# Longer rows for w_mod, w_gate and the last 4 MB of w_o in a decode layer whose loads never stop

## The chip, the cores and the metric

The kernel runs on one core of a Trainium2 chip. The metric is the device time of one execution in microseconds (us), median over runs. "Span" is the profiled execution from its first to its last instruction, some 1.4 us less than the device time (436.2 us at 437.56, before).

## The reference, cut to what matters

One token goes through one transformer layer: adaLN modulation, attention with 32 query heads and 4 cached key/value heads of 65,536 positions, and a gated feed-forward network.

```python
# x, c: (1, 1024); w_mod: (1024, 6144); wq: (1024, 4096); wo: (4096, 1024)
# k_cache, v_cache: (4, 65536, 128); w_gate, w_up: (1024, 3584); w_down: (3584, 1024); all bf16
mod = silu(c) @ w_mod                       # six vectors sa, ca, ga, sb, cb, gb
h = layernorm(x) * (1 + ca) + sa
x = x + ga * (attention(h @ wq, k_cache, v_cache) @ wo)
h = layernorm(x) * (1 + cb) + sb
return x + gb * ((gelu(h @ w_gate) * (h @ w_up)) @ w_down)
```

The arithmetic is small. What has to be moved is not: 67 MB of K, 67 MB of V and 51 MB of weights, 185.6 MB in all, each byte read once.

## The kernel before

All large loads go through one queue (SyncE) into ten slots of 16 KB per partition. A load is planned with the slots it takes; `issue_ready` sends the loads off in their order, each as soon as the last users of its slots are done. Nearly every load has a partition's bytes as one contiguous run in memory, called a row below (some of w_down are two): a load of 2 k-rows of w_mod is 128 rows of 24 KB.

```python
    def plan_load(src, view_fn, slot, site=None, nslot=1, beside=None, off=0, sem=None):

        if site is not None:
            site.n += 16
            tok = (site.sem, site.n)
        else:
            sem = slot if sem is None else sem
            nfill[sem] += 1
            tok = (fill[sem], 16 * nfill[sem])
        job = Job(view_fn(slot_all[:, slot * SLOT + off:(slot + nslot) * SLOT]), tok, slot)
        job.src = src
        job.freed = None
        job.prev = []
        if beside is not None:
            job.prev = beside.prev
        for t in range(slot, slot + (nslot if beside is None else 0)):
            if last_job[t] is not None and last_job[t] not in job.prev:
                job.prev.append(last_job[t])
            last_job[t] = job
        loads.append(job)
        return job

    # ... (cut)

    def issue_ready():

        while issued[0] < len(loads):
            j = loads[issued[0]]
            if any(q.freed is None for q in j.prev):
                return
            SP.wait(*(q.freed for q in j.prev))
            sp.dma_start(j.view, j.src).then_inc(j.tok[0], 16)
            issued[0] += 1
# ... (cut)
        head = iter([8, 0, 2, 4, 6, 8])
        j_mod = [(plan_load(wmod_v[:, k:k + 2, :], flat(2, M6), next(head), nslot=2), k, 2) for k in range(0, KD, 2)]
        j_q = [(plan_load(wq_v[:, k:k + 4, :], flat(4, HQ * DH), next(head), nslot=2), k, 4) for k in range(0, KD, 4)]
        tail = iter([2, 4, 6, 8])
        tail_d = iter([0, 1, 2, 3, 4, 5])

        def plan_o(k, slot):
            return (plan_load(wo_v[:, k:k + 8, :], flat(8, D), slot), k, 8)
        # ... (cut: K and V in loads of 4 MB, 128 rows of 32 KB)
        j_o += [plan_o(16, 0), plan_o(24, 1)]
        j_g = [(plan_load(wg_v[:, k:k + 4, :], flat(4, F), next(tail), nslot=2), k, 4) for k in range(0, KD, 4)]
        j_u = [(plan_load(wu_v[:, k:k + 4, :], flat(4, F), next(tail), nslot=2), k, 4) for k in range(0, KD, 4)]
```

w_mod is four loads, wq two, w_o four, w_gate two. wq's second half takes the slots of w_mod's first piece. K then goes to slots 0 to 3 and V to slots 4 to 7. Slot 5 is read once before anything of V has landed (multiplied by zeros), so the part of it that w_mod does not cover is cleared by a memset on GpSimd.

The matrix products with weights all go through one helper. It waits for one load, does all matmuls on it, and releases the slots:

```python
        def row_matvec(place, jobs, pad, ready, last_k, between=None):

            PE.wait(*ready)
            tok = None
            seen = set()
            for n, (jb, view, k0, nk) in enumerate(jobs):
                PE.wait(jb.tok)
                ins = None
                for kk in range(nk):
                    k = k0 + kk
                    for out, c0 in place(k):
                        ins = pe.matmul(
                            out, pad[:, k, :], view[:, kk, c0:c0 + ROW],
                            start=k <= last_k[0], stop=k >= last_k[1], skip_group_check=True,
                        )
                tok = PE.done(ins)
                release(jb, tok)
                if n == 0 and between is not None:
                    between()
            return tok
```

Of the kernel before, what the change touches and what calls it, by code (L numbers as in the profile page):

```python
# [10 lines left out]
SLOT = 8192  # L11
NSLOT = 10
SITES = 4
# [5 lines left out]
UE = 4  # L19
# [61 lines left out]
def bass_adaLN_cond__gqa_block_cached__geglu_ffn__decode_kernel(  # L81
# [14 lines left out]
    D = A_x.shape[-1]  # L96
    KD = D // P
# [6 lines left out]
    F = B_w_gate.shape[1]  # L104
    FD = F // P
    M6 = w_mod.shape[1]
# [4 lines left out]
    NB = CH // TB  # L111
    scale = float(DH) ** -0.5
    NQ = P // QD
    assert FD % UE == 0 and M6 <= SLOT and KD % 4 == 0
    assert REP * NB == QD and NB == NQ and CH == NB * NQ * (ROW // P) and HQ == QD
    assert D == 2 * ROW and HQ * DH == 2 * NQ * ROW and F % ROW == 0 and F <= 2 * NQ * ROW and UE * P == ROW

# [5 lines left out]
    sp, pe, dve, act, pool = nc.sync, nc.tensor, nc.vector, nc.scalar, nc.gpsimd  # L123
# [68 lines left out]
    slots = [slot_all[:, i * SLOT:(i + 1) * SLOT] for i in range(NSLOT)]  # L192
# [7 lines left out]
# [21 lines that stand above are left out]
# [20 lines left out]
    def flat(nk, n):  # L241
        return lambda t: t[:, 0:nk * n].rearrange("p (k n) -> p k n", k=nk)

    def emit_all():
# [3 lines left out]
        wmod_v = w_mod.rearrange("(p k) n -> p k n", p=P)  # L248
        wq_v = A_wq.rearrange("(p k) n -> p k n", p=P)
        wo_v = A_wo.rearrange("(p k) n -> p k n", p=P)  # L250
        wg_v = B_w_gate.rearrange("(p k) n -> p k n", p=P)
# [5 lines left out]
        def kv_src(h, i, n=1):  # L257
            g, cc = divmod(i, NCH)
            return h[g][:, cc * CH:(cc + n) * CH, :]

        head = iter([8, 0, 2, 4, 6, 8])
        j_mod = [(plan_load(wmod_v[:, k:k + 2, :], flat(2, M6), next(head), nslot=2), k, 2) for k in range(0, KD, 2)]
        j_q = [(plan_load(wq_v[:, k:k + 4, :], flat(4, HQ * DH), next(head), nslot=2), k, 4) for k in range(0, KD, 4)]
        tail = iter([2, 4, 6, 8])
        tail_d = iter([0, 1, 2, 3, 4, 5])

        def plan_o(k, slot):
            return (plan_load(wo_v[:, k:k + 8, :], flat(8, D), slot), k, 8)

        def vslot(j):  # L270
            return SITES + j % SITES
# [10 lines left out]
        j_o = []  # L282
        for i in range(0, NC + KU, KU):
            if i < NC:
                j_k[i] = plan_load(kv_src(kh, i, KU), flat(KU * CH, DH), i % SITES, kfill[i % SITES // KU], KU)
            if i == SITES - KU:
                j_o.append(plan_o(0, 8))
            if i == NC:
                j_o.append(plan_o(8, 9))
            if i >= KU:  # L290
                j = i - KU
                j_v[j] = plan_load(kv_src(vh, j, VU), flat(VU * CH, DH), vslot(j), vfill[j % SITES // VU], VU)
        j_o += [plan_o(16, 0), plan_o(24, 1)]
        j_g = [(plan_load(wg_v[:, k:k + 4, :], flat(4, F), next(tail), nslot=2), k, 4) for k in range(0, KD, 4)]
        j_u = [(plan_load(wu_v[:, k:k + 4, :], flat(4, F), next(tail), nslot=2), k, 4) for k in range(0, KD, 4)]
        j_d = []
        NBF = FD // UE
# [43 lines left out]
        pool.memset(p_row[:, :, :], 0.0)  # L341
        pool.memset(p_sb[:, :, :], 0.0)
        pool.memset(m_sp[:, :, :], 0.0)
        pool.memset(slots[SITES + 1][:, 2 * M6 - SLOT:SLOT], 0.0)
        for a in [a for r in ev for a in r] + ex + m1 + oc + pc + kfill + vfill:
            pool.sem_inc(a.sem, a.unit)
        v_zero = GP.done(pool.memset(kt_sb[:, 1, :, :], 0.0))
# [531 lines left out]
        assert issued[0] == len(loads)  # L879

    emit_all()
    return nc

# [27 lines left out]
```

## Time and profile before

| | before |
|---|---|
| device time | 437.57 us (3 runs, 437.57 to 437.58) |
| span of the profiled run | 436.2 us |
| bytes on the load queue | 185.60 MB in 8176 packets |
| busy: TensorE, DVE, ScalarE | 69%, 47%, 26% |
| DMA engines | 99.0% of the span under load packets |

The page's lines are quoted and read in the prediction below. Two habits of reading help here. First, the DMA row is in tenths per slice, so a 9 means 90% or more, and the row under it, GB/s, shows what moved. Second, a load counts as landed when the last of 16 DMA engines has reported. The views show that last report ("us to landing", or the end of a wait). For the last piece of w_mod it comes at 32.69 us, and the matmuls that wait for it start at 32.73. With 128 rows to a load, that is 8 rows for each engine, and the last reports of the four pieces of w_mod (10.92, 18.18, 25.44 and 32.69 us) are 7.25 or 7.26 us apart, about 8 times the 0.912 us that one of their packets takes.

### The profile page before, as it was taken

Reading aid. Unit: us, or ns where it says so; the run is one execution under the profiler, and the core shown is the slowest. Engines: PE = TensorE matmul, PEld = TensorE weight load, DVE = VectorE, ACT = ScalarE, POOL = GpSimd, SP = SyncE. Lnnn points to the kernel's source line nnn. Section 1 sums busy time; section 2 is a strip of 40 time slices with the busy share of each in tenths; the row PEclk is TensorE's granted clock in tenths of the full one; section 3 lists DMA queues with packets and bytes.
Section 4 is the critical chain, followed back from the end, with each engine's and each line's share of the span. In section 5 each row is a group of like instructions: output and inputs, shape, how many; then the busy total and the mean of one; then the engine's idle time right before and its main releaser. Section 6 shows DMA issues by size and latency. Waiting matters only on the chain.

```text
span 436.2 us, 8423 instructions
## 1 busy us (share of the span) xinstructions
PE 302.8 (69%) x3858; PEld 200.5 (46%) x3858; DVE 206.7 (47%) x303; ACT 111.2 (26%) x164; POOL 16.8 (4%) x23
## 2 busy tenths in 40 slices
PE   0435559959696878949787794969689596565366
PEld 0112236736464656636465563646456373232024
DVE  6601015637373755736474763738377465321001
ACT  1000001533332423333341353333235334000000
POOL 9500000000000000000000000000000000000000
PEclk9995569999796988988896897969689889578856
DMA  8999999999999999999999999999999999999996
GB/s 355 433 421 434 433 431 431 431 432 433 433 433 439 430 433 433 436 433 433 439 433 433 433 430 436 433 436 436 433 433 433 433 418 436 437 433 429 420 425 265
DMA packets 8192, 185.77 MB, mean 426 GB/s; under 512 B 1010, under 2 KB 1010, under 8 KB 1652
## 3 DMA queue, kind: packets, MB, share of 16 engines
q1 hardware_dynamic: 8176, 185.60, 99.0%
q8 instruction: 8, 0.13, 0.1%
q14 instruction: 4, 0.03, 0.0%
q10 hardware_dynamic: 4, 0.00, 0.0%
HBM read 185.60 MB, written 0.00 MB: 426 GB/s over the span
## 4 chain that ended last, share of the span: by engine, by line
DMA 56%; PE 31%; DVE 11%; issue 1%; ACT 1%; POOL 0%; POOLq 0%
DMA slots<-in_A_k_cache_dram 45%; PE kt_ps L575 16%; DMA slots<-in_B_w_down_dram 7%; PE b L645 4%; DMA slots<-in_A_v_cache_dram 4%; PE sc_ps L597 4%; PE kt_ps L409 3%; DVE selt L359 3%; DVE kt_sb L683 2%; DVE s_pad L717 1%; DVE o_red L706 1%; PE sc_ps L626 1%; PE b L613 1%; PE b L386 1%; DVE o_acc L694 1%
## 5 line engine op out<-in xcount | busy, mean ns | idle before, releaser
L575 PE MATMUL kt_ps<-ident,slots 128*128 128x128 bf16 x2048 | 156.7, 238 | 48.8 <-DMA slots<-in_A_k_cache_dram 48.0
L683 DVE COPY kt_sb<-kt_ps 128x2048 bf16<-128x2048 bf16 x96 | 117.6, 1225 | 111.5 <-PE kt_ps L575 109.9
L575 PEld LDWEIGHTS kt_ps<-ident,slots 128*128 128x128 bf16 x2048 | 136.1, 108 | 74.3 <-issue 41.9
L683 ACT ACTIVATE kt_sb<-kt_ps 128x2048 bf16<-128x2048 bf16 x32 | 60.1, 1877 | 27.7 <-PE kt_ps L575 27.7
L732 ACT ACTIVATE p_sb<-sc_ps 128x512 bf16<-128x512 bf16 x32 | 19.1, 597 | 182.4 <-PE sc_ps L626 182.4
L597 PE MATMUL sc_ps<-kt_sb,q_buf 128*32 128x512 bf16 x528 | 50.8, 420 | 0.0
L645 PE MATMUL b<-slots,p_sb 128*32 128x512 bf16 x560 | 40.1, 411 | 5.3 <-DMA slots<-in_A_v_cache_dram 4.6
L409 PE MATMUL kt_ps<-slots,h_pad 128*32 128x512 bf16 x176 | 19.1, 571 | 22.0 <-DMA slots<-in_B_w_up_dram 9.7
L694 DVE SCALAR_TENSOR_TENSOR o_acc<-o_acc,s_pad,b 128x512 f32<-128x512 f32 x28 | 20.9, 747 | 12.2 <-PE b L645 11.9
L613 PE MATMUL b<-m_sp,selt 128*128 128x16 f32 x66 | 13.0, 272 | 18.2 <-DVE m_sp L722 16.5
L645 PEld LDWEIGHTS b<-slots,p_sb 128*32 128x32 bf16 x560 | 15.5, 104 | 20.1 <-issue 5.1
L717 DVE TENSOR_REDUCE s_pad<-sc_ps 128x1 f32<-128x512 f32 x32 | 21.8, 682 | 0.0
L738 ACT ACTIVATE p_row<-sc_ps,s_pad 128x512 bf16<-128x512 f32 x32 | 21.7, 677 | 0.0
L409 PEld LDWEIGHTS kt_ps<-slots,h_pad 128*32 128x32 bf16 x176 | 6.3, 130 | 32.7 <-issue 11.9
L613 PEld LDWEIGHTS b<-m_sp,selt 128*128 128x128 f32 x66 | 9.8, 188 | 23.7 <-DVE m_sp L722 21.4
L597 PEld LDWEIGHTS sc_ps<-kt_sb,q_buf 128*32 128x32 bf16 x528 | 10.9, 95 | 12.3 <-issue 4.5
L409 PE MATMUL kt_ps<-slots,s_pad 128*32 128x512 bf16 x96 | 10.9, 516 | 7.5 <-DMA slots<-in_w_mod_dram 7.5
L452 POOL TENSOR_TENSOR rs<-va,halfneg 128x1 f32<-128x1 f32 x2 | 1.1, 555 | 375.7 <-DVE va L449 375.7
L793 DVE COPY kt_sb<-kt_ps 128x512 f32<-128x512 f32 x3 | 2.1, 692 | 27.7 <-PE kt_ps L409 27.7
L626 PEld LDWEIGHTS sc_ps<-ident,p_row 128*128 128x128 bf16 x136 | 7.8, 98 | 15.1 <-issue 14.4
L626 PE MATMUL sc_ps<-ident,p_row 128*128 128x128 bf16 x136 | 13.7, 224 | 0.2 <-ACT p_row L738 0.2
L727 DVE TENSOR_REDUCE s_pad<-b 128x1 f32<-128x16 f32 x32 | 5.6, 175 | 14.6 <-PE b L613 14.6
(98 smaller groups left out, 148.1 us busy)
## 6 DMA issues: line engine op xcount, KB each, us to landing
slots<-in_A_k_cache_dram SPq DMA_DIRECT2D x16, 4096.0 KB, 23.5
slots<-in_A_v_cache_dram SPq DMA_DIRECT2D x16, 4096.0 KB, 23.6
slots<-in_w_mod_dram SPq DMA_DIRECT2D x4, 3072.0 KB, 20.4
slots<-in_A_wq_dram SPq DMA_DIRECT2D x2, 4096.0 KB, 35.8
slots<-in_A_wo_dram SPq DMA_DIRECT2D x4, 2048.0 KB, 25.3
slots<-in_B_w_gate_dram SPq DMA_DIRECT2D x2, 3584.0 KB, 30.2
slots<-in_B_w_up_dram SPq DMA_DIRECT2D x2, 3584.0 KB, 29.5
slots<-in_B_w_down_dram SPq DMA_DIRECT2D x2, 2048.0 KB, 35.1
```

Of the source, the lines that this page charges most:

```text
L359: dve.tensor_scalar(selt[:, :].rearrange("p (r h) -> p r h", h=REP), selw[:, HQ - REP:HQ].unsqueeze(1).to_broadcast([P, NR, REP]), -scale, ...
L409: ins = pe.matmul(out, pad[:, k, :], view[:, kk, c0:c0 + ROW], start=k <= last_k[0], stop=k >= last_k[1], skip_group_check=True,)
L575: ins = pe.transpose(kt_ps[:, half * 2048 + t * P:half * 2048 + (t + 1) * P], j_k[i - i % KU].view[:, i % KU * CH + b * TB + t, :], ident[ ...
L597: ins = pe.matmul(sc(j)[QD * g:QD * (g + 1), :], q_buf[:, j % SITES, QD * b:QD * (b + 1)], kt_sb[:, j % 2, n:n + w, :].rearrange("p n d -> ...
L613: ins = pe.matmul(b6[:, 0:NR], selt[:, :], m_sp[:, j % 2, :], start=True, stop=True)
L626: ins = pe.transpose(sc_bf[:, o:o + P], p_row[:, j % 2, c * P:(c + 1) * P], ident[:, :])
L645: ins = pe.matmul(b7[QD * c:QD * (c + 1), :].rearrange("p (b d) -> p b d", b=NB), p_sb[:, s, c * P + QD * g:c * P + QD * (g + 1)], v[:, NQ ...
L683: ev[i % SITES][b].done(act.activation(dst, src, ACT.Copy) if E_ is AC else dve.tensor_copy(dst, src))
L694: v = oc[j % SITES].done(dve.scalar_tensor_tensor(o_acc[:, :], o_acc[:, :], al[:, j:j + 1], b7[:, :], ALU.mult, ALU.add))
L717: v = DVE.done(dve.tensor_reduce(m_new, sc(j), AX.X, ALU.max))
L732: pc[jt % SITES].done(act.activation(p_sb[:, jt % SITES, :], sc_bf[:, o:o + ROW], ACT.Copy))
L738: v_x[j] = ex[s].done(act.activation(p_row[:, j % 2, :], sc(j), ACT.Exp, bias=mneg[:, j:j + 1], scale=scale, accum_out=zr[:, j:j + 1],))
```

## The change

Its intent is to have the same bytes moved by fewer, longer rows and fewer DMAs. w_mod becomes two loads of 48 KB rows, w_gate one of 56 KB, and the last 4 MB of w_o one of 32 KB. With w_mod in slots 0 to 5, wq no longer has to wait for a slot, and the memset of slot 5 is not needed.

```diff
--- before.py
+++ after.py
@@ -111,7 +111,7 @@
     NB = CH // TB
     scale = float(DH) ** -0.5
     NQ = P // QD
-    assert FD % UE == 0 and M6 <= SLOT and KD % 4 == 0
+    assert FD % UE == 0 and 4 * M6 == 3 * SLOT and KD % 4 == 0 and KD * F <= 4 * SLOT
     assert REP * NB == QD and NB == NQ and CH == NB * NQ * (ROW // P) and HQ == QD
     assert D == 2 * ROW and HQ * DH == 2 * NQ * ROW and F % ROW == 0 and F <= 2 * NQ * ROW and UE * P == ROW
 
@@ -258,14 +258,14 @@
             g, cc = divmod(i, NCH)
             return h[g][:, cc * CH:(cc + n) * CH, :]
 
-        head = iter([8, 0, 2, 4, 6, 8])
-        j_mod = [(plan_load(wmod_v[:, k:k + 2, :], flat(2, M6), next(head), nslot=2), k, 2) for k in range(0, KD, 2)]
+        head = iter([0, 3, 6, 8])
+        j_mod = [(plan_load(wmod_v[:, k:k + 4, :], flat(4, M6), next(head), nslot=3), k, 4) for k in range(0, KD, 4)]
         j_q = [(plan_load(wq_v[:, k:k + 4, :], flat(4, HQ * DH), next(head), nslot=2), k, 4) for k in range(0, KD, 4)]
-        tail = iter([2, 4, 6, 8])
+        tail = iter([6, 8])
         tail_d = iter([0, 1, 2, 3, 4, 5])
 
-        def plan_o(k, slot):
-            return (plan_load(wo_v[:, k:k + 8, :], flat(8, D), slot), k, 8)
+        def plan_o(k, slot, n=8):
+            return (plan_load(wo_v[:, k:k + n, :], flat(n, D), slot, nslot=n // 8), k, n)
 
         def vslot(j):
             return SITES + j % SITES
@@ -290,8 +290,8 @@
             if i >= KU:
                 j = i - KU
                 j_v[j] = plan_load(kv_src(vh, j, VU), flat(VU * CH, DH), vslot(j), vfill[j % SITES // VU], VU)
-        j_o += [plan_o(16, 0), plan_o(24, 1)]
-        j_g = [(plan_load(wg_v[:, k:k + 4, :], flat(4, F), next(tail), nslot=2), k, 4) for k in range(0, KD, 4)]
+        j_o.append(plan_o(16, 0, 16))
+        j_g = [(plan_load(wg_v, flat(KD, F), 2, nslot=4), 0, KD)]
         j_u = [(plan_load(wu_v[:, k:k + 4, :], flat(4, F), next(tail), nslot=2), k, 4) for k in range(0, KD, 4)]
         j_d = []
         NBF = FD // UE
@@ -341,7 +341,6 @@
         pool.memset(p_row[:, :, :], 0.0)
         pool.memset(p_sb[:, :, :], 0.0)
         pool.memset(m_sp[:, :, :], 0.0)
-        pool.memset(slots[SITES + 1][:, 2 * M6 - SLOT:SLOT], 0.0)
         for a in [a for r in ev for a in r] + ex + m1 + oc + pc + kfill + vfill:
             pool.sem_inc(a.sem, a.unit)
         v_zero = GP.done(pool.memset(kt_sb[:, 1, :, :], 0.0))
```

## The prediction

0.28 us for packets and 0.04 us for completions, 0.31 us before rounding, take 437.57 us to 437.26. In the paragraph with the packet sizes, "its packet records" are those of the trace; the trace has 512 packets of 24 KB for the 4 x 128 rows of w_mod, so one packet is one row. Rival A is that each DMA has a fixed cost that shows in the time when four are saved; the figure for it is cut, as no run shows it (section 3 measures about 7 ns per DMA). The 435.2 GB/s in the answer to it are 16 engines at the 27.2 GB/s of the packet line.

> **What bounds the kernel now.** I read the page first, from its table of slices to its chain, then the issues with their landing times, then the DMA queue's own waits, then the timelines of the head (0 to 70 us) and of the tail (363 to 436 us). The page:
>
> ```profile
> span 436.2 us, 8423 instructions
> ...
> PE 302.8 (69%) x3858; PEld 200.5 (46%) x3858; DVE 206.7 (47%) x303; ACT 111.2 (26%) x164; POOL 16.8 (4%) x23
> ...
> DMA  8999999999999999999999999999999999999996
> GB/s 355 433 421 434 433 431 431 431 432 433 433 433 439 430 433 433 436 433 433 439 433 433 433 430 436 433 436 436 433 433 433 433 418 436 437 433 429 420 425 265
> DMA packets 8192, 185.77 MB, mean 426 GB/s; under 512 B 1010, under 2 KB 1010, under 8 KB 1652
> ...
> q1 hardware_dynamic: 8176, 185.60, 99.0%
> ...
> DMA 56%; PE 31%; DVE 11%; issue 1%; ACT 1%; POOL 0%; POOLq 0%
> ```
>
> No compute engine is over 69%, but the DMA row is full from the first slice to the last but one, and the load queue's packets (q1) cover 99.0% of 16 engines' span, 431.8 us per engine. The chain of waits names matmuls of many lines, but it goes through transfers where it matters (56% of the span). So this is one stream of 185.60 MB that starts near 1.75 us (first packet on q1) and ends near 433.1 us (last one), with a short tail after it. Whether its supply ever runs thin, the queue's own waits and the issue times tell:
>
> ```profile
> SPq L231 <- PE b L645: 159.3, 18, 19.9
> SPq L231 <- PE kt_ps L575: 149.4, 15, 12.5
> SPq L231 <- PE kt_ps L409: 74.5, 9, 28.4
> ```
>
> SyncE waits nearly all the time for slots. That looks alarming and is not: a K or V load of 4 MB needs 9.7 us at 433 GB/s but lands 23.5 us after its issue (median), so about 1.4 loads lie ahead of it whenever it is issued. The queue never drains.
>
> [...] the issues overlap, and consecutive K landings keep a pace of 38.72 us for two K and two V loads (K waits end at 116.05, 154.70, 193.41, 232.14 us), 16.78 MB at 433.3 GB/s, with no pause per DMA. [...] Its packet records have medians of 84 ns for 2 KB, 159 for 4 KB, 309 for 8 KB, 611 for 16 KB, 912 for 24 KB, 1062 for 28 KB and 1213 for 32 KB. These lie on one line: 8.7 ns plus bytes over 27.2 GB/s (24 KB: 903.5 + 8.7 = 912.2). One packet is one contiguous row, so a longer row saves 8.7 ns and nothing else. [...] The landings here follow the issue order, so an issue that is later but still ahead of its turn costs nothing.
>
> **The change part by part.**
>
> Packets. w_mod goes from 4 x 128 rows of 24 KB to 2 x 128 of 48 KB: 256 fewer. w_gate from 2 x 128 of 28 KB to 128 of 56 KB: 128 fewer. The last 4 MB of w_o from 2 x 128 of 16 KB to 128 of 32 KB: 128 fewer. Together 512, or 32 per engine; 32 x 8.7 ns = 0.28 us. Four DMAs fewer also means four completion packets fewer per engine, of 9 ns each in the records: 0.04 us. All of it is on the path, since the stream has no gap: 0.31 us.
>
> Head, SyncE and PE. The landings before, each as issue plus time to landing, are 10.9, 18.1, 25.5 and 32.7 us for the four w_mod pieces.
>
> ```profile
> 17.96 5.36 PE L409 MATMUL kt_ps<-slots,s_pad 128*32 128x512 bf16 x48
> ...
> 25.48 1.90 PE L409 MATMUL kt_ps<-slots,s_pad 128*32 128x512 bf16 x24 [2.15 <-DMA slots<-in_w_mod_dram]
> ...
> 32.73 3.60 PE L409 MATMUL kt_ps<-slots,s_pad 128*32 128x512 bf16 x24 [5.34 <-DMA slots<-in_w_mod_dram]
> ...
> 43.23 3.60 PE L409 MATMUL kt_ps<-slots,h_pad 128*32 128x512 bf16 x32 [3.60 <-DMA slots<-in_A_wq_dram]
> ...
> 52.79 3.29 PE L409 MATMUL kt_ps<-slots,h_pad 128*32 128x512 bf16 x32 [4.88 <-DMA slots<-in_A_wq_dram]
> ...
> 62.54 1.89 PE L575 MATMUL kt_ps<-ident,slots 128*128 128x128 bf16 x16 [4.56 <-DMA slots<-in_A_k_cache_dram]
> ```
>
> The first large piece holds what the first two held, so it lands at about 18.1 us. Its 48 matmuls end near 23.4 us as they do now, and the first K load, which needs those slots, is issued near 23.4 us as now (23.36). The second large piece lands at 32.7 and leaves 48 matmuls instead of 24; at the half clock granted there (24 in 3.60 us) that is 7.2 us, to 39.9 instead of 36.3. The chain from there to h_pad takes 4.1 us (36.33 to 40.39), so it is ready at 44.0, where wq's first half has landed at 43.2: 0.8 us late. The 4.88 us wait for wq's second half swallows it. The second K load is issued at 39.9 instead of 27.7 us, but its turn in the queue comes only at 62.5. The second half of wq no longer waits for slots (it was issued near 21.6 us); its turn comes near 42 us, so that is worth nothing either.
>
> The memset that goes:
>
> ```profile
> 4.58 11.99 DVE L359 TENSOR_SCALAR selt<-selw 128x128 f32<-128x128 f32 x1
> ...
> 6.11 3.50 POOL L344 MEMSET slots<- 128x4096 bf16 x1
> ...
> 9.57 6.91 POOL L347 MEMSET kt_sb<- 128x8192 bf16 x1
> ```
>
> DVE hangs from 4.58 to 16.57 us and goes on just when GpSimd's two last memsets end. Without 3.50 us of memset, s_pad is ready at about 13.8 instead of 17.3 us. But PE then waits for the large piece until 18.1. Worth 0 to the end.
>
> Tail. w_gate lands whole at 399.2 us, where its second half lands now.
>
> ```profile
> 394.09 3.31 PE L409 MATMUL kt_ps<-slots,h_pad 128*32 128x512 bf16 x28 [2.03 <-DVE h_pad L464]
> ...
> 399.22 1.91 PE L409 MATMUL kt_ps<-slots,h_pad 128*32 128x512 bf16 x28 [1.82 <-DMA slots<-in_B_w_gate_dram]
> ...
> 407.69 3.34 PE L409 MATMUL kt_ps<-slots,h_pad 128*32 128x512 bf16 x28 [4.56 <-DMA slots<-in_B_w_up_dram]
> ```
>
> The bracket at the end of a line is the idle time before it and what ended it. The 28 matmuls that ran at 394 now run behind 399.2: 56 matmuls, 3.3 + 1.9 = 5.2 us, to 404.4 instead of 401.1. The copies and turn that follow (401.18 to 403.13) end at 406.4. PE waits for w_up until 407.69 anyway: 1.3 us of the 4.56 remain. If all 56 run at half clock (6.7 us), it ends at 407.9, 0.2 us late, which the 5.15 us wait for w_up's second half takes up. The w_down loads that need w_gate's slots are issued from 404.4 instead of 397.4 us, those in w_o's slots at 388.8 instead of 387.9; then w_up and 4 MB of w_down are still ahead in the queue, over 9 MB or 20 us. w_gate's issue needs four slots, the last of which is freed at 365.8; until 381.9 the queue has w_o.
>
> Sum: 0.28 + 0.04, 0.31 before rounding, off the stream, 0 elsewhere; 437.57 - 0.31 = 437.26 us. After the stream's end at 433.1 come the last w_down matmuls and 2 us of sum, store and wait; they start from landings and move with them.
>
> **The rivals.** (A) [...] Against it: the 433.3 GB/s above with 32 KB rows, and a stream so full that 435.2 GB/s would itself only give 426.5 us for the bytes; all overheads together are about 5.3 us of the 431.8[...]. (B) Coarser pieces make a hole in the stream: a late issue of the second K load, of w_gate or of w_down. For it: three issues move by 0.9 to 12 us. Against it: each has 16 us or more of queued transfers ahead. A hole would cost its length, 1 to 3 us, to 439 or 440. (C) Rows over 32 KB are cut again when descriptors are made, or run at another rate. No row so long is in this trace. Cut in two, only w_o's 128 packets and the four completions go: 0.11 us, so 437.46; cut at 24 and 28 KB is the same. (D) The end is set by PE, not by the stream:
>
> ```profile
> 431.14 3.14 PE L386 MATMUL b<-p_row,slots 128*128 128x1 bf16 x48
> ```
>
> The last 48 matmuls run back to back at a granted clock of 0.5 to 434.28, while the last packet landed at 433.1 and 8 matmuls take 0.5 us: PE is some 0.6 us behind the stream. If its clock falls otherwise, the tail moves by up to 0.6 us, most likely to the better, as it is already at half: 436.7 to 437.6.
>
> **Range and chances.** The gain rests on a slope that seven sizes share, its place on a gapless stream. What is open is row size (C, up to +0.2), the tail's clock and the place of the eight 16 KB instruction fetches among the engines (D, -0.6 to +0.3). So 437.26, eight in ten from 436.75 to 437.65. 2% is 8.75 us; neither A nor B gets there. Faster 0.01, within 0.98, slower 0.01.
>
> **What would show it.** Right: q1 has 7600 packets (8176 - 512 - 64), the under-512 B count is 946; 48 KB packets take near 1.816 us and 56 KB ones 2.117; the first K transpose starts near 62.4 us; the waits for w_up and for wq's second half shrink but stay; the GB/s row is unchanged; the memset line is gone and DVE's hang ends near 13 us. Wrong: more packets than that (C); a slice in the middle or at 390 to 430 us under 415 GB/s (B); PE without a wait between w_gate and the end (B or D); an end that moves by more than the last landing does (D).

## The result and the profile after

| | before | after |
|---|---|---|
| device time, the rounds of this comparison | 437.57 us (437.43 to 437.63, 6 runs) | 437.65 us (437.28 to 437.94, 6 runs) |
| ratio, after over before | | 1.0001, 95% interval 0.9989 to 1.0014 |
| all runs, mean and standard deviation | 437.55, 0.10 (38 runs) | 437.67, 0.25 (16 runs) |

A ratio is the mean time of one kernel's fast runs over that of the other's of the same rounds, so it isn't quite the ratio of the medians. The two kernels take the same time. The forecast saving of 0.31 us is not there. Over all runs the changed kernel is 0.12 us slower in the mean, not clear of its own scatter, and its scatter is more than twice that of the kernel before.

The page after, the lines that answer to those of before:

```profile
span 436.4 us, 8418 instructions
...
DMA  9999999999999999999999999999999999999996
GB/s 362 433 415 437 433 434 431 428 432 433 433 433 433 433 436 436 439 433 433 436 433 433 433 433 433 436 433 436 433 433 436 433 415 451 437 438 415 422 421 254
DMA packets 7617, 185.77 MB, mean 426 GB/s; under 512 B 947, under 2 KB 947, under 8 KB 1589
...
q1 hardware_dynamic: 7600, 185.60, 98.9%
```

The load queue has the 7600 packets that were forecast, and is as full as before. No slice in the middle has a hole. So the rows were not cut again, and the stream was not starved.

The timeline of the head after (start in us, duration in us, engine, line, operation; in brackets the idle time before it and what ended that):

```profile
4.58 8.53 DVE L358 TENSOR_SCALAR selt<-selw 128x128 f32<-128x128 f32 x1
...
18.01 5.13 PE L408 MATMUL kt_ps<-slots,s_pad 128*32 128x512 bf16 x48 [3.42 <-DMA slots<-in_w_mod_dram]
...
32.48 6.41 PE L408 MATMUL kt_ps<-slots,s_pad 128*32 128x512 bf16 x48 [9.34 <-DMA slots<-in_w_mod_dram]
...
43.33 1.91 PE L408 MATMUL kt_ps<-slots,h_pad 128*32 128x512 bf16 x32 [1.95 <-DMA slots<-in_A_wq_dram]
...
52.90 3.60 PE L408 MATMUL kt_ps<-slots,h_pad 128*32 128x512 bf16 x32 [6.64 <-DMA slots<-in_A_wq_dram]
...
62.64 1.89 PE L574 MATMUL kt_ps<-ident,slots 128*128 128x128 bf16 x16 [3.37 <-DMA slots<-in_A_k_cache_dram]
```

DVE gets free 3.5 us earlier, and TensorE then waits 3.42 us for the larger piece. The second half of w_mod ends at 38.9 us instead of 36.3, and the wait for wq takes that up. The first K work starts at 62.64 us, where it started at 62.54 before and 62.4 was forecast. The tail after:

```profile
399.50 5.53 PE L408 MATMUL kt_ps<-slots,h_pad 128*32 128x512 bf16 x56 [7.53 <-DMA slots<-in_B_w_gate_dram]
...
407.84 1.91 PE L408 MATMUL kt_ps<-slots,h_pad 128*32 128x512 bf16 x28 [0.82 <-DMA slots<-in_B_w_up_dram]
...
431.28 3.18 PE L385 MATMUL b<-p_row,slots 128*128 128x1 bf16 x48
```

The whole of w_gate is worked off in 5.53 us, and 0.82 us of the wait for w_up are left. So every wait is where the prediction put it, and still all of the tail is 0.14 us later than before (the last group started at 431.14). Something in the stream itself has eaten the saving.

The 16 reports of the last w_down load show what. This is worked out from the trace's semaphore records, in us from the span's start:

```
                     first   mean of 16   last   last - mean   span
before               431.60    432.56    433.40     0.84      436.2
after                431.39    432.47    433.54     1.07      436.4
```

The first engine is done 0.21 us earlier and the mean 0.09 us earlier, but the last is 0.14 us later, and the end follows the last. This gave the theory that the experiments had to test. **Theory S**: per engine the stream did get shorter, by less than forecast, but the end is set by the slowest of the 16 engines, and the change made that one lag more. **Rivals**: the end is set by TensorE or some later wait (P); longer rows save nothing (N).

### The profile page after: what moved, and what is told of

The parts are those of the page before. It is cut to its first block, busy times and chain, and to the rows that moved or that the text cites. A ratio compares the mean times of both kernels' runs of the same rounds, so it can differ in the third digit from the quotient of the medians.

```text
span 436.4 us, 8418 instructions
## 1 busy us (share of the span) xinstructions
PE 301.9 (69%) x3858; PEld 200.4 (46%) x3858; DVE 203.2 (47%) x303; ACT 111.2 (25%) x164; POOL 13.4 (3%) x22
## 4 chain that ended last, share of the span: by engine, by line
DMA 61%; PE 30%; DVE 7%; issue 0%; ACT 0%
DMA slots<-in_A_k_cache_dram 44%; PE kt_ps L574 16%; DMA slots<-in_B_w_gate_dram 8%; DMA slots<-in_B_w_down_dram 5%; PE sc_ps L596 5%; PE b L644 4%; DMA slots<-in_w_mod_dram 4%; DVE kt_sb L682 3%; PE kt_ps L408 3%; DVE s_pad L716 1%; PE b L612 1%; DVE o_red L705 1%; PE b L385 1%; PE sc_ps L625 1%; DVE o_acc L693 1%; DVE m_sp L721 1%
## 5 line engine op out<-in xcount | busy, mean ns | idle before, releaser
L644 PE MATMUL b<-slots,p_sb 128*32 128x512 bf16 x560 | 42.3, 429 | 5.6 <-DMA slots<-in_A_v_cache_dram 4.9
L408 PE MATMUL kt_ps<-slots,h_pad 128*32 128x512 bf16 x176 | 16.6, 513 | 23.5 <-DMA slots<-in_A_wq_dram 8.6
L408 PEld LDWEIGHTS kt_ps<-slots,s_pad 128*32 128x32 bf16 x96 | 4.2, 126 | 19.7 <-DMA slots<-in_w_mod_dram 13.3
```

What stands on the lines that cost most here:

```text
L408: ins = pe.matmul(out, pad[:, k, :], view[:, kk, c0:c0 + ROW], start=k <= last_k[0], stop=k >= last_k[1], skip_group_check=True,)
L644: ins = pe.matmul(b7[QD * c:QD * (c + 1), :].rearrange("p (b d) -> p b d", b=NB), p_sb[:, s, c * P + QD * g:c * P + QD * (g + 1)], v[:, NQ ...
```

## The experiments

Twelve runs were made, all correct, each of five rounds, four runs at a time on one chip beside the kernel before. Some repeat a kernel. The table has the measured figures of all; "difference" is the mean of a kernel's runs minus that of the kernel before in the same rounds. The last three columns are from the 16 reports of the profiled run (that of "more instruction fetches" is its fastest run, 458.06 us).

| kernel | median us | difference us | mean landing | last landing | last - mean |
|---|---|---|---|---|---|
| before (first profile) | 437.57 | | 432.56 | 433.40 | 0.84 |
| before again | 437.48 | -0.08 | 432.53 | 433.44 | 0.91 |
| after (first profile) | 437.65 | +0.06 | 432.47 | 433.54 | 1.07 |
| after again | 437.50 | -0.02 | 432.43 | 433.37 | 0.94 |
| after, third | 437.90 | +0.27 | 432.42 | 433.73 | 1.31 |
| head only | 437.97 | +0.37 | 432.58 | 433.83 | 1.25 |
| head only again | 437.73 | +0.17 | 432.56 | 433.73 | 1.17 |
| tail only | 437.42 | -0.11 | 432.46 | 433.33 | 0.87 |
| K and V in 2 MB loads | 438.95 | +1.38 | 434.03 | 434.83 | 0.80 |
| split K and V rows | 438.71 | +1.17 | 433.75 | 434.60 | 0.85 |
| after, short first rows | 437.29 | -0.20 | 432.39 | 433.25 | 0.86 |
| the same again | 437.32 | -0.28 | 432.36 | 433.18 | 0.83 |
| head only, short first rows | 437.54 | -0.07 | 432.51 | 433.33 | 0.83 |
| more instruction fetches | 459.46 | +21.75 | 448.36 | 453.99 | 5.63 |

### 1. The changed kernel again

No edit.

> The changed kernel once more. Theory S (slowest engine): the packets take 0.3 us less per engine as predicted, but the last landing is that of the slowest of 16 engines, whose lag is set by how the engines start and by which of them also fetch instructions; so the time scatters by some tenths of a us about a mean 0.1 to 0.3 us under the kernel before, and within each profile the time follows the last landing of the last w_down load (span = last landing + 2.8 us), while the mean landing over 16 engines stays near 432.47 us (kernel before: 432.56). Rival P (the end is set by TensorE or by a later wait): the distance from last landing to the end grows over 2.8 us. Rival N (no saving at all): time equal to before, 437.5 to 437.7 us, and the mean landing not under that of before.

It took 437.50 us (437.38 to 437.92), ratio 1.0000 (0.9986 to 1.0014). Its last landing was at 433.37 us and its span 436.16 us, so 2.79 us lay between; before it had been 2.78. Over all profiles of the table this distance is 2.68 to 2.81 us. Rival P falls: the end is a fixed time after the last landing. The mean landing, 432.43 us, is under that of before, so rival N falls too. One forecast of theory S failed: a mean time 0.1 to 0.3 us under the kernel before. It was 0.02 us under it here and 0.27 us over it in the third set. The lag of the slowest engine is what differs from run to run.

### 2. The head of the change alone, and the tail alone

```diff
# head only (on the kernel before; an assert that goes with it is cut)
-        head = iter([8, 0, 2, 4, 6, 8])
-        j_mod = [(plan_load(wmod_v[:, k:k + 2, :], flat(2, M6), next(head), nslot=2), k, 2) for k in range(0, KD, 2)]
+        head = iter([0, 3, 6, 8])
+        j_mod = [(plan_load(wmod_v[:, k:k + 4, :], flat(4, M6), next(head), nslot=3), k, 4) for k in range(0, KD, 4)]
-        pool.memset(slots[SITES + 1][:, 2 * M6 - SLOT:SLOT], 0.0)
# tail only: the w_o and w_gate lines of the change, and none of these
```

> Only w_mod and the slots of wq as in the change. 16 packets and 2 completions per engine fewer: 0.16 us by the packet line. Theory S with a start cost: the first packet of each engine takes 0.78 us more than the line says with 48 KB rows (0.53 with 24 KB), so 0.25 us of it are given back, and the time is 437.5 to 437.8 us. Without a start cost that depends on the row: 437.3 to 437.5 us.

> Only w_gate and w_o as in the change, head as before. 16 packets and 2 completions per engine fewer: the mean landing falls by 0.16 us, and the first packets have the excess of before, 0.53 us. Theory S: 437.2 to 437.6 us, the scatter of the slowest engine over it. Rival P (the whole w_gate makes TensorE late): 437.7 us or more.

The head alone took 437.97 us (437.81 to 438.08): slower than forecast by either theory, though with 16 packets fewer per engine. Its mean landing did not fall (432.58 us), and its slowest engine lagged by 1.25 us. The start cost in its expectation was read from one profile each; over all profiles, the first 16 load packets take 0.67 to 0.78 us more in the mean than the line says with 48 KB rows, and 0.53 to 0.70 us with 24 KB. The tail alone took 437.42 us (437.35 to 437.67), 0.11 us less than before in the mean; its mean landing fell by 0.1 us to 432.46 and its lag was that of before. The intervals of both ratios hold 1 (0.9996 to 1.0023 and 0.9984 to 1.0011), so these are differences of means; they agree with the landings.

Repeated on another chip, the head alone:

> The head of the change alone, once more, beside its variant with short first rows on one chip. 437.8 to 438.1 us if the 0.4 us belong to the kernel; 437.4 to 437.7 if they belonged to the chip or to chance. In its profile, last minus mean landing is 1.0 us or more in the first case.

It took 437.73 us (437.35 to 438.08), 0.17 us over the kernel before, with a lag of 1.17 us. This lies between the two forecasts, and one of its five runs was as fast as the kernel before, so the time alone doesn't decide. The sign is the same, and the lag is over the 1.0 us forecast for a cost that belongs to the kernel.

### 3. What a packet costs

The forecast took 8.7 ns per packet from packet durations. Two kernels add 4096 packets each, 256 per engine. In the first, K and V come in loads of 2 MB, so there are also 32 more DMAs:

```diff
-KU = 2
-VU = 2
+KU = 1
+VU = 1
-        for j in (-2 * VU, -VU):
+        for j in range(-LAG, 0, VU):
```

> The kernel before with K and V in loads of 2 MB with rows of 16 KB: 4096 packets more, 256 per engine at 8.7 ns, and 32 more DMAs at 9 ns: 2.2 + 0.3 = 2.5 us. Theory S and the packet line: 440.1 us (439.6 to 440.6), 12272 + 512 packets on the load queue. Rival N (a packet's fixed cost is hidden behind its neighbour): 437.4 to 437.8 us. [...]

```profile
span 437.6 us, 8476 instructions
...
DMA packets 12801, 185.78 MB, mean 425 GB/s; under 512 B 1522, under 2 KB 1522, under 8 KB 2164
...
q1 hardware_dynamic: 12784, 185.61, 99.3%
```

In the second, a load of 4 MB is made of two chunks that don't adjoin in memory, so only the rows change, not the number of DMAs:

```diff
# (cut: the destination is viewed in the same two chunks when the load is issued)
-            return h[g][:, cc * CH:(cc + n) * CH, :]
+            h4 = h[g].rearrange("p (t c m) d -> p c t m d", t=n, m=CH)
+            return h4[:, cc // n, :, :, :]
```

> The kernel before, with each K and V load of 4 MB made of two chunks that don't adjoin in memory: as many DMAs and bytes, but rows of 16 KB, so 256 packets more per engine and nothing else. Theory D (a packet costs the 8.7 ns that its duration has over its bytes): +2.2 us, 439.8. Theory O (neighbouring packets overlap by about half of that; what counts is the pace, some 4.3 ns, as the run with loads of 2 MB suggests once 9 ns are taken off per DMA): +1.1 us, 438.6 to 438.8. Theory Q (the 1.35 us of the run with 2 MB loads were its 32 further DMAs at 40 ns): no change, 437.4 to 437.7.

```profile
span 437.4 us, 8423 instructions
...
DMA packets 12288, 185.77 MB, mean 425 GB/s; under 512 B 1010, under 2 KB 1010, under 8 KB 1652
...
q1 hardware_dynamic: 12272, 185.60, 99.2%
```

The two pages tell that the dose arrived: 12,784 and 12,272 packets instead of 8176, in the second with as many packets under 512 B (the completions) as before. The times are 438.95 us (+1.38, ratio 1.0032, 1.0018 to 1.0045) and 438.71 us (+1.17, ratio 1.0027, 1.0013 to 1.0040). So a packet costs 1.17 us / 256 = 4.6 ns of the stream, about half of what its duration says, and a DMA in a full queue (1.38 - 1.17) / 32 = 7 ns. The second figure is rough: it rests on 0.2 us between two chips, where 0.1 us is chance (section 4). The first kernel's forecast of 440.1 us was wrong by much the same factor; the second's (theory O: 438.6 to 438.8) was right, and theories D and Q fall. The missing 4 ns fit packets that overlap with their neighbours on an engine, which was not shown, as the records don't name the engine. Either way, the durations of this stream's packets add up to too much: 32 packets of 1213 ns and 4 completions of 9 ns make 38.85 us per engine for two K and two V loads, which landed in 38.72 us.

### 4. What makes an engine lag

The kernel before against itself shows the ground level:

> The kernel before against itself: what the method shows where there is no difference. 437.4 to 437.7 us, ratio 1.000; mean landing of the last w_down load 432.5 to 432.6 us, last landing 0.8 to 0.9 us after the mean.

437.48 us (437.31 to 437.55), ratio 0.9998, lag 0.91 us. A difference of 0.1 us between five runs and the others of a kernel is chance.

The 16 reports of successive loads, sorted and counted from the first of each load, show when the lag arises. From the profile of the changed kernel with short first rows (described below), where it is plainest; beside it, the times at which the packet records show a 16 KB fetch of instructions:

```
first report   the six slowest engines, us behind the first      16 KB fetches up to then
   31.76       0.13 0.20 0.22 0.24 0.36 0.62                     none
   41.45       0.26 0.27 0.29 0.42 0.59 1.67                     36.4
   70.48       0.21 0.23 0.25 0.53 1.62 1.92                     64.5
   75.34       0.27 0.29 0.54 1.59 1.90 1.94                     75.3
   85.04       0.25 0.50 1.55 1.75 1.86 1.91                     84.9
   94.73       0.49 1.58 1.64 1.71 1.73 1.82                     93.2
```

With each fetch one more engine is found 1.5 to 1.9 us behind the first, and it stays back. The records don't name the engine, so the pairing is read from the counts: 0, 1, 2, 3, 4, 5. The packet records bear it out. In this profile ten load packets after 35 us last over 0.1 us longer than the line says, and each of them starts within 15 ns of the end of one of the ten fetches between 35 and 431 us (seven of 16 KB, three of 8 KB from another instruction queue, q14). A 16 KB fetch (0.89 to 0.96 us) and what it adds to that packet (0.46 to 0.55 us) make 1.43 us. The 16 KB fetches are the eight of the instruction queue q8 on every page; three more come at 388, 410 and 431 us. At the end, eight of the 16 engines are 1.4 us or more behind the first: as many as the seven 16 KB fetches before 431 us and one engine set back by 8 KB fetches. Where the end is late, the sorted reports can be read as those of an engine that was late at the start and also had a fetch (section 5).

To test that fetches do this in time as well, 4096 semaphore increments that nobody waits for were given to GpSimd, which has nothing to do in mid-stream (in the profile before, one of its waits lasts 373.5 us):

```diff
         hn1, v_hn1 = ln_norm(x_col, v_c, 32)
+        pad_sems = [nc.alloc_semaphore(f"pad{i}") for i in range(8)]
+        for i in range(4096):
+            pool.sem_inc(pad_sems[i % 8], 1)
```

> The kernel before, with 4096 semaphore increments that nobody waits for on the otherwise idle GpSimd, so that some 256 KB of instructions more are fetched in mid-stream. Theory F (each fetch holds up one of the 16 engines by its own transfer and some more, 0.3 to 0.6 us for 8 KB, and the slowest engine sets the end): about 32 fetches more on the instruction queues; mean landing +0.6 to +1.2 us, time 438.1 to 439.5 us. Rival (fetches slip in for nothing): 437.4 to 437.7 us.

Before, from the DMA view:

```profile
q8 instruction: 8, 0.13, 0.1%
q14 instruction: 4, 0.03, 0.0%
...
slots<-in_A_k_cache_dram SPq DMA_DIRECT2D x16, 4096.0 KB, 23.5
```

With the increments:

```profile
span 456.8 us, 12519 instructions
...
GB/s 345 446 442 420 438 427 418 447 416 443 423 437 434 423 448 414 423 437 411 428 426 400 385 386 434 402 400 405 382 425 346 442 298 416 435 439 419 414 421 95
...
q1 hardware_dynamic: 8176, 185.60, 96.1%
q14 instruction: 36, 0.29, 0.2%
```

There are 32 fetches more (q14 had 4) with 0.26 MB, 8 KB each, as forecast, but the time rose by 21.75 us instead of 0.6 to 2. The number was missed because I had spread the fetches over the engines. They did not spread. In the reports, one engine alone falls back: by 4.2 us at 70 us, 6.2 at 104, 8.7 at 143, that is 0.69 us per fetch (2.57 us between 104 and 143 us, with a fetch each 10.3 us), while the other 15 are where they were before (first report at 143.17 us, before 143.21). At 241 us its lag has reached 13.9 us and grows no more. That is about the reserve in the queue, the 1.4 loads of 9.7 us that the prediction read from the issue times. From there on the other 15 engines run dry and wait, since each next load needs slots that the slowest engine has not filled: the GB/s row falls to 298 to 442 in the slices after, and between 348 and 382 us the DMA engines are busy for 0.89 of the time, before 1.00. 32 fetches of 0.69 us are 22 us on that one engine, and that is nearly what the whole kernel lost (20.6 us at the last landing of this profile). So the sum, too, is that of the slowest engine. The increments were not tried without their fetches, but little is left for them: of the 0.69 us per fetch, the packet records hold 0.64, namely 0.31 us of the fetch and 0.33 us that the load packet right behind it lasts longer.

### 5. Short first rows

The start differs as well. At the last w_mod landing, before any 16 KB fetch, the distances from the first of the 16 engines to the 15th and to the 16th are as follows (the profile with more fetches is left out):

```
first rows    to the 15th (us)              to the 16th (us), same order
12 KB         0.36 0.32 0.43                0.62 0.92 0.75
24 KB         0.44 0.54 0.48 0.40 0.44      0.91 0.85 0.64 0.89 0.79
48 KB         0.67 0.55 0.73 0.72 0.62      0.75 0.72 0.95 0.87 0.68
```

Up to the 15th, the engines start further apart with longer rows; with the 16th counted, the three rows overlap.

**Theory G**: with long first rows the engines start further apart, and what they lose to fetches comes on top. To test it, the changed kernel got a short first load. w_mod's first piece is cut into 12 KB rows and 36 KB rows in the same slots; all else stays:

```diff
-        j_mod = [(plan_load(wmod_v[:, k:k + 4, :], flat(4, M6), next(head), nslot=3), k, 4) for k in range(0, KD, 4)]
+        s0 = next(head)
+        j_mod, jb = [], None
+        for k, n in ((0, 1), (1, 3)):
+            jb = plan_load(wmod_v[:, k:k + n, :], flat(n, M6), s0, nslot=3, beside=jb, off=k * M6, sem=k)
+            j_mod.append((jb, k, n))
+        for t in range(3):
+            last_job[s0 + t] = jb
+        j_mod.append((plan_load(wmod_v[:, 4:8, :], flat(4, M6), next(head), nslot=3), 4, 4))
```

> The changed kernel, but its first piece of w_mod in two loads into the same three slots: first rows of 12 KB, then of 36 KB; the rest as in the change. Per engine 24 packets and 3 completions fewer than before: 0.13 us by the pace of packets. Theory G (long first rows make the 16 engines start further apart, and the slowest sets the end): the spread of the engines in the first landings shrinks to that of before or less, the last landing is 0.9 us or less after the mean, and the time is 437.2 to 437.45 us, under the changed kernel. Rival (the lag of the slowest engine has nothing to do with the first rows): 437.5 to 437.9 us, last minus mean 0.95 to 1.25.

It took 437.29 us (437.23 to 437.50), as forecast. The kernel before took 437.51 us in these rounds; the changed kernel was not run on this chip. The lag is 0.86 us, the mean landing 432.39. The tail of its timeline:

```profile
430.99 3.12 PE L392 MATMUL b<-p_row,slots 128*128 128x1 bf16 x48
...
434.54 0.35 SPq L883 DMA_DIRECT2D out_dram<-kt_sb  x1
```

The last group of matmuls starts 0.29 us before that of the changed kernel (431.28) and 0.15 us before that of the first kernel (431.14).

The same edit on the head alone tells theory G from the other novelties of the head (later issue of the second K load, no memset, other slots):

> The head of the change alone, with its first piece of w_mod cut in rows of 12 KB and then of 36 KB. Theory G (the head alone took 0.4 us more because long first rows set the 16 engines further apart at the start, and the slowest one, held up by an instruction fetch on top, ends the stream): the engines' first landings lie within 0.4 to 0.6 us instead of 0.87, last minus mean at the end is 0.8 to 0.9 instead of 1.25 us, and the time is 437.35 to 437.6 us. Rival H (the later issue of the second K load, the removed memset or the other slots cost the time): 437.8 to 438.1 us, as the head alone.

It took 437.54 us (437.37 to 437.56) beside 437.73 of the head alone on the same chip, with a lag of 0.83 us instead of 1.17. One of the five runs of the head alone (437.35) is under all of these, so it is the lag more than the time that speaks. The slots, the missing memset and the late K load are all still there, so rival H falls. The forecast for the start failed: the first landings lie within 0.75 us, not 0.4 to 0.6. Beside them, the last two runs of that chip:

> The changed kernel a third time, beside the two head kernels. Theory G: 0.1 us under the head alone for its longer rows in the tail, so 437.4 to 437.9 us, with more scatter than the kernel before.

> The changed kernel with first rows of 12 KB and 36 KB once more. If it beats both kernels: 437.2 to 437.45 us, 0.1 to 0.3 us under the kernel before of the same rounds, and under the changed kernel of the same call.

The changed kernel took 437.90 us (437.42 to 438.10), its lag 1.31 us; in the mean that is 0.11 us over the head alone, where 0.1 us under it was forecast. With short first rows it took 437.32 us (437.22 to 437.35), a mean of 0.28 us under the kernel before (437.60 median of those rounds), and all five runs of it are below all nine of the kernel before. So this version lies under both kernels, by 0.06% under the first (ratio 0.9994, 0.9980 to 1.0008; the interval holds 1). Over both calls it took 437.31 us in the mean (10 runs, standard deviation 0.08).

That shorter first rows take the extra lag away is shown; how they do it is not. Theory G's spread does not order the profiles once the 16th engine is counted. The sorted reports, followed by their values, suggest another reading. In all eight profiles with first rows of 12 or 24 KB, the engine that starts last still stands 0.5 to 0.9 us behind the first at about 94 us, so none of the first five 16 KB fetches set it back. In all five with 48 KB its place is empty by then, and one engine is found 2.0 to 2.4 us behind, about its 0.6 to 0.9 us and 1.4 us of a fetch. So it may count which engine starts last, rather than how far apart they start. No run changes the one without the other.

## Why the prediction was right or wrong, point by point

**Right: the bound.** One stream of loads sets the time, the parts of the change that move waits are worth nothing, and the total stays within 2%. The page after has the forecast 7600 packets (947 under 512 B; 946 forecast, and one packet of 96 B on an instruction queue falls into the span). The packet records show 1815 ns for a 48 KB row and 2116 for one of 56 KB; 1816 and 2117 were forecast. The measured 437.65 us is at the upper edge of the range, and that it is inside is partly luck: two terms of the sum were wrong, the forecast saving did not come, and the third set of rounds gave 437.90 us.

**Right: the waits.** The memset's 3.50 us went into the wait for the larger first piece (3.42 us). w_mod's second half ended at 38.9 us, forecast 39.9 (the 48 matmuls took 6.41 us, and 0.15 us for each was too much); h_pad was ready before wq's first half landed instead of 0.8 us after. The second K load was issued at 38.93 us, forecast 39.9. w_gate's 56 matmuls took 5.53 us, forecast 5.2, and left 0.82 us of wait, forecast 1.3. Rivals A and B did not come to pass: with four DMAs fewer the time did not fall (437.65 us, before 437.57), and there is no hole. C neither: no row was cut.

**Wrong: the 8.7 ns per packet.** "32 x 8.7 ns = 0.28 us" is the step. A packet's duration has 8.7 ns over its bytes, but the pace of the stream pays only about half of that: the dose of 256 packets alone measured 4.6 ns. With 7 ns per DMA the saving per engine is 32 x 4.6 + 4 x 7 = 175 ns, 0.17 us instead of 0.31. The prediction had what it needed for a better figure: it took a sum of durations and did not check that against the pace of the stream it had quoted. 32 KB at 27.2 GB/s are 1204.7 ns; 38.72 us for 32 packets and 4 completions are 1210 per packet, so 5.3 ns for a packet and an eighth of a completion.

**Wrong: "All of it is on the path, since the stream has no gap."** The saving is a mean over 16 engines, and the end follows the slowest. In the three profiles of the changed kernel the mean landing is 432.44 us, in the two of before 432.55: a gain of 0.11. The lag is 1.11 us in the mean, before 0.88: a loss of 0.23. Together that makes +0.12 us, and the times over all runs differ by +0.12. The lag comes from the head alone (1.25 and 1.17 us against 0.87 for the tail alone) and goes away with short first rows (0.86, 0.83, 0.83). Rival D named the place of the instruction fetches among the engines as open, and looked for it in the range, not in the change. That the change itself would alter how the engines start was not thought of.

**Open.** Why long first rows make the slowest engine later is not shown, only that they do: by a wider start or by another engine that starts last. Of the mean gain, 0.06 us of the 0.17 are missing. They seem to go at the start too: at the last w_mod landing the mean of the 16 reports is 32.03 us with first rows of 24 KB (six profiles) and 31.98 with 48 KB (five), a gain of 0.05 where the measured costs of packet and DMA give 0.09; with 12 KB (three) it is 31.92. At this size that is a reading of a few profiles. Which engine gets a fetch is not in the records.

## What to carry to other kernels

In this kernel the saving per DMA engine did not show in the time, since the slowest engine did not have it (the mean landing came 0.11 us earlier, the lag grew by 0.23 us), so look at all 16 completion reports of a load, not at the last. Take a packet's cost from the pace of a stream, or from a dose of some thousand packets more (4.6 ns, from 4096 packets); the durations of this stream's packets added up to too much (8.7 ns). In this full stream, one row less per DMA engine was worth under 5 ns, and the first load was better with short rows: the slowest engine ended 0.83 to 0.86 us after the mean with rows of 12 KB, 0.80 to 0.91 with 24 KB, 0.94 to 1.31 with 48 KB.
